# A queue of its own for gelu's derivative in a convolution and joint-network training step

## The chip, the cores and the metric

One core of a Trainium2 chip. The time is that of one execution on the device, in microseconds, host not counted. Engines: PE multiplies matrices (PEld loads its weights), DVE (VectorE) and ACT (ScalarE) work on elements, POOL (GpSimd) does so too and issues some DMAs, SP issues the others. PE writes to PSUM, which DVE and ACT empty ("evict").

## The reference

A small speech network, forward and backward. The forward part, cut to what matters:

```python
h = conv1d(x, w1, taps=3);  h = gelu(h)[:, ::2]      # T = 16000 -> 8000
f = conv1d(h, w2, taps=3);  f = gelu(f)[:, ::2]      # 8000 -> 4000
fe = f @ w_f                                         # [2, 4000, 256]
ge = g @ w_g                                         # [2, 8, 256]
j = tanh(fe[:, :, None, :] + ge[:, None, :, :])      # [2, 4000, 8, 256]
out = j @ w_o
```

`jax.vjp` then gives the gradients of all seven inputs for a given `grad_out`. Inputs and outputs are bfloat16, D = V = 256. gelu is the tanh approximation. The kernel computes it as x * sigmoid(A * (x + K x^3)) with s for the sigmoid, and its derivative as s + h * (1 - s) * (A + 3 A K x^2), where h is gelu's value.

## The kernel before, in words

**Tiling.** The 4000 time steps of the joint network are cut into chunks of 512 (`CW`), 8 per batch row, the last 416 wide, so 16 chunks in all, `n` = 0 to 15. Elements lie with the feature dimension on the 128 partitions in two halves (`KT` = 2), time along the free dimension. Because the second half of every gelu's output is thrown away, one chunk needs the first convolution at two of four input phases (`par` 0 and 1) and the second at one: three gelus a chunk, each 128 x 1024 elements.

**Order of the work.** The main loop runs over chunks. In iteration n four pairs of `u` (`up`) do the joint network of chunk n: `joint_units` gives out its work in small units. `weave` steps through these and, at a `ratio` of 0.85 units per step (0.28 in chunk 0), draws units from `fill`, a list that holds the forward half of chunk n+1 (`conv_units`, `conv2_units`, `fe_units`) and the backward half of chunk n-1 (`d1_units`, `d5_units`, `gwf_units`, `gw2_units`, `e_units`). The fill's order is: the first convolution with d1 between, d5 with gwf and gw2, then `conv2_units`, six units of e, `fe_units`, the rest of e.

**The gelu (line 196).** `gelu` returns two lists of instructions and issues none. `first` makes h: x*x, times K, (.+1)*x, the sigmoid on ACT, s*x into HT (first convolution) or FT (second). `second` makes the derivative in five DVE operations: g_sq = 3A*g_sq + A; g_x = 1 - s; g_sq *= g_x; g_sq *= h; G = g_sq + s, with G1 or G2 as the result. So g_x, g_sq and g_s live until the derivative is done. All these show as line 194 in the profile.

**The queue `later` (line 189).** The lists go into one queue, `later`, and `pump(2)`, called at each step of `weave`, issues two operations of it. For the first convolution the two `first` lists come before all ten `second` operations, with two small POOL copies of G1's border column behind (lines 259 and 263). `conv2_units` and `fe_units` begin by emptying the queue (lines 270 and 297). For chunk 0, worked in halves so that it starts sooner, the derivatives wait in a list `seconds0` and enter `later` behind the second convolution.

**Who uses the derivative.** G2 of chunk n-1 is read in iteration n by line 339 (GF), G1 by line 370 (GH). Both exist since iteration n-2. G1 and G2 have two buffers each.

**Buffers.** The pool `gel` has two of each of g_x, g_sq and g_s. `outp` has three OUT tiles of 4 KB per partition, filled by ACT (line 626) and sent by a POOL DMA (line 653) once a pair of u. `rowp` has six tiles, used by the backward transposes and, in chunk 0, by the second convolution's scratch. PSUM has seven buffers `ps` for everything but the accumulator GWO_ps.

**Other lines that matter.** 532: NGZ on DVE, out of PSUM; 524: ACT's square JSQ (two buffers), which 532 reads; 551: POOL's sum over u, ACCN and at the end NGFE; 323: DVE adds weight gradients out of PSUM (ACC); 383: copies of transposes out of PSUM (rows, JR); 313: ACT's tanh; 482: ACT's GX; 303: PE's product FE from FT.

The program is written as a stream of instructions on named tiles. The framework puts in all waits, gives out buffers, and sets the order on each engine, by the order of emission and by when it takes an instruction to be ready; engines then run in order. Only `keep_in_program_order` pins an instruction.

Of the kernel before, what the change touches and what calls it, by code (L numbers as in the profile page):

```python
# [13 lines left out]
BF16 = mybir.dt.bfloat16  # L14
FP32 = mybir.dt.float32
ALU = mybir.AluOpType
# [5 lines left out]
P = 128  # L22
KT = 2
# [4 lines left out]
CW = 512  # L28
# [3 lines left out]
def kernel(  # L32
# [22 lines left out]
    nc = tc.nc  # L55
# [7 lines left out]
    def geom(n):  # L63
        b, ci = chunks[n]
        c0 = ci * CW
        return b, ci, c0, min(CW, MQ - c0)
# [4 lines left out]
    pool = lambda name, bufs, **kw: ctx.enter_context(tc.tile_pool(name=name, bufs=bufs, **kw))  # L71
    const = pool("const", 1)
    xcp = pool("xcp", 6)
    gel = pool("gel", 2)
    htp = pool("htp", 3)
    g1p = pool("g1p", 2)
    ftp = pool("ftp", 2)
# [12 lines left out]
    jsp = pool("jsp", 2)  # L90
    ngzp = pool("ngzp", 3)
    jrp = pool("jrp", 3)
    outp = pool("outp", 3)
    tailp = pool("tailp", 1)
    PS = bass.MemoryType.PSUM
    psp = pool("psp", 7, space=PS)
# [2 lines left out]
    def ps_f32():  # L99
        return psp.tile([P, 512], FP32, name="ps", tag="ps")  # L100
# [24 lines left out]
    S = [dict() for _ in range(G)]  # L125
# [57 lines left out]
    def scratch(name, spare):  # L183
        if spare:
            return rowp.tile([P, 8, P], BF16, name="rows")[:].rearrange("p (k a) b -> p k (a b)", k=KT)
        return gel.tile([P, KT, CW], BF16, name=name)


    later = deque()

    def pump(k):
        for _ in range(k):
            if later:
                later.popleft()()  # L194

    def gelu(xb, W, h, gp, off, kts=((0, KT),), spare=False):

        sq, s = scratch("g_sq", spare), scratch("g_s", spare)
        TT, TS, STT = nc.vector.tensor_tensor, nc.vector.tensor_scalar, nc.vector.scalar_tensor_tensor
        first, second = [], []  # L200
        for (k0, k1) in kts:
            sq_, s_, x_ = sq[:, k0:k1, :W], s[:, k0:k1, :W], xb[:, k0:k1, :W]
            h_, gp_ = h[:, k0:k1, off:off + W], gp[:, k0:k1, off:off + W]
            first += [
                partial(TT, out=sq_, in0=x_, in1=x_, op=ALU.mult),
                partial(TS, out=sq_, in0=sq_, scalar1=GELU_K, scalar2=None, op0=ALU.mult),
                partial(STT, out=s_, in0=sq_, scalar=1.0, in1=x_, op0=ALU.add, op1=ALU.mult),
                partial(nc.scalar.activation, out=s_, in_=s_, func=ACT.Sigmoid, scale=GELU_A),
                partial(TT, out=h_, in0=s_, in1=x_, op=ALU.mult),
            ]  # L210
            second += [
                partial(TS, out=sq_, in0=sq_, scalar1=3.0 * GELU_A, scalar2=GELU_A, op0=ALU.mult, op1=ALU.add),
                partial(TS, out=x_, in0=s_, scalar1=-1.0, scalar2=1.0, op0=ALU.mult, op1=ALU.add),
                partial(TT, out=sq_, in0=sq_, in1=x_, op=ALU.mult),
                partial(TT, out=sq_, in0=sq_, in1=h_, op=ALU.mult),
                partial(TT, out=gp_, in0=sq_, in1=s_, op=ALU.add),
            ]
        return first, second


    HALVES = ((0, 1), (1, 2))

    seconds0 = []

    def conv_units(n):
        b, ci, c0, W = geom(n)
        seconds = []
        st = S[n]
        HT = htp.tile([P, 2, KT, CW + 2], BF16, name="HT")
        G1 = g1p.tile([P, 2, KT, CW + 2], BF16, name="G1")  # L230
        st["HT"], st["G1"] = HT, G1
        if ci == 0:
            nc.gpsimd.memset(HT[:, 1, :, 1:2], 0.0)
        else:
            nc.gpsimd.tensor_copy(out=HT[:, 1, :, 1:2], in_=S[n - 1]["HT"][:, 1, :, CW + 1:CW + 2])
        taps = {0: ((1, 0, 0), (2, 1, 0), (0, 3, -1)), 1: ((0, 1, 0), (2, 3, 0), (1, 2, 0))}
        for par in range(2):
            xb = gel.tile([P, KT, CW], BF16, name="g_x")
            for mt in range(KT):
                ps = ps_f32()  # L240
                k = 0
                for (i, c, sh) in taps[par]:
                    for kt in range(KT):
                        nc.tensor.matmul(ps[:, :W], lhsT=W1[:, i, kt, mt * P:(mt + 1) * P],  # L244
                                         rhs=st["X", c][:, kt, 16 + sh:16 + sh + W], start=(k == 0), stop=(k == 5))
                        k += 1
                nc.scalar.copy(out=xb[:, mt, :W], in_=ps[:, :W])
                yield
            first, second = gelu(xb, W, HT[:, par], G1[:, par], 2, HALVES if n == 0 else ((0, KT),))
            later.extend(first)  # L250
            seconds += second
            if n == 0:
                pump(len(first))
        if n == 0:
            seconds0.extend(seconds)
        else:
            later.extend(seconds)
        if ci > 0:
            later.append(lambda: nc.gpsimd.tensor_copy(out=G1[:, :, :, 1:2], in_=S[n - 1]["G1h"][:]))
        if ci < NCH - 1:  # L260
            st["G1h"] = halo.tile([P, 2, KT, 1], BF16, name="G1h")
            (seconds0 if n == 0 else later).append(
                lambda: nc.gpsimd.tensor_copy(out=st["G1h"][:], in_=G1[:, :, :, CW + 1:CW + 2]))

    def conv2_units(n):
        b, ci, c0, W = geom(n)
        st = S[n]
        HT = st["HT"]
        if n > 0:
            pump(len(later))  # L270
        FT = ftp.tile([P, KT, CW], BF16, name="FT")
        G2 = ftp.tile([P, KT, CW], BF16, name="G2")
        st["FT"], st["G2"] = FT, G2
        xb = scratch("g_x", n == 0)
        for mt in range(KT):
            ps = ps_f32()
            k = 0
            for (i, par, off) in ((1, 0, 2), (0, 1, 1), (2, 1, 2)):
                for kt in range(KT):
                    nc.tensor.matmul(ps[:, :W], lhsT=W2[:, i, kt, mt * P:(mt + 1) * P],  # L280
                                     rhs=HT[:, par, kt, off:off + W], start=(k == 0), stop=(k == 5))
                    k += 1
            nc.scalar.copy(out=xb[:, mt, :W], in_=ps[:, :W])  # L283
            yield
        first, second = gelu(xb, W, FT, G2, 0, HALVES if n == 0 else ((0, KT),), n == 0)
        if n == 0:
            for f in first:
                f()
            seconds0[:0] = second
            later.extend(seconds0)  # L290
        else:
            later.extend(first + second)

    def fe_units(n):
        b, ci, c0, W = geom(n)
# [386 lines left out]
    def weave(main, fill, ratio):  # L682

        due = 0.0
        for _ in main:
            pump(2)
            due += ratio
            while due >= 1.0:
                due -= 1.0
                if next(fill, StopIteration) is StopIteration:  # L690
                    due = -1e9
# [65 lines left out]
    for _ in chain(warm(16), small_units(), conv_units(0), transposed_units(), warm(4), conv2_units(0), warm(16), fe_units(0)):  # L757
        pass
# [4 lines left out]
    for n in range(G):  # L763
# [27 lines left out]
        for up in range(U // 2):  # L791
# [17 lines left out]
            if up == U // 2 - 1:  # L809
                for _ in fill:  # L810
                    pump(2)
                pump(len(later))
    n = G - 1
    gwo_rest(*prev_gwo[0], 0)
    for (o, M) in blocks(window(n)[1] - window(n)[0]):
# [2 lines left out]
        pass  # L818


    fin = gel
    for i in range(KK):
        t_ = fin.tile([P, 512], BF16, name="g_sq", tag="g_sq")
        nc.scalar.copy(out=t_[:], in_=ACC1[:, i, :])
        nc.sync.dma_start(out=out_2[i].rearrange("(dt p) n -> p dt n", p=P), in_=t_[:].rearrange("p (k n) -> p k n", k=KT))
        t_ = fin.tile([P, 512], BF16, name="g_s", tag="g_s")
        nc.vector.tensor_copy(out=t_[:], in_=ACC2[:, i, :])
        nc.sync.dma_start(out=out_3[i].rearrange("(dt p) n -> p dt n", p=P), in_=t_[:].rearrange("p (k n) -> p k n", k=KT))
    t_ = fin.tile([P, 512], BF16, name="g_x", tag="g_x")
    nc.vector.tensor_scalar(out=t_[:], in0=ACCF[:], scalar1=-1.0, scalar2=None, op0=ALU.mult)  # L830
    nc.sync.dma_start(out=out_5.rearrange("(dt p) n -> p dt n", p=P), in_=t_[:].rearrange("p (k n) -> p k n", k=KT))
    t_ = fin.tile([P, 512], BF16, name="g_x", tag="g_x")
    nc.scalar.copy(out=t_[:], in_=GWO_ps[:].rearrange("p k v -> p (k v)"))
    nc.sync.dma_start(out=out_7.rearrange("(dt p) n -> p dt n", p=P), in_=t_[:].rearrange("p (k n) -> p k n", k=KT))

# [2 lines left out]
                            in_=NGGEc[:].rearrange("p b k u c -> p (b k u) c"),  # L838
# [4 lines left out]
    for b in range(B):  # L843
# [11 lines left out]
        for dt in range(KT):  # L855
            nc.tensor.matmul(GWG_ps[:, dt * D:(dt + 1) * D], lhsT=GR8[:, b, dt * P:(dt + 1) * P],
                             rhs=ngR[:].rearrange("u kt p -> u (kt p)"),
                             start=(b == 0 and dt == 0), stop=(b == B - 1 and dt == KT - 1))
    t_ = fin.tile([P, 512], BF16, name="g_sq", tag="g_sq")
    nc.scalar.activation(out=t_[:], in_=GWG_ps[:], func=ACT.Copy, scale=-1.0)  # L860
    nc.sync.dma_start(out=out_6.rearrange("(dt p) n -> p dt n", p=P), in_=t_[:].rearrange("p (k n) -> p k n", k=KT))

# [29 lines left out]
```

## Time and profile before

| | |
|---|---|
| median of 3 runs | 883.72 us (882.99 to 883.83) |
| profiled execution | 882.75 us, of which the span is 881.0 us |
| PE, DVE, ACT, POOL busy | 833.0, 678.9, 639.0, 419.6 us |
| L194 on DVE, x*x (49 times) | 58.2 us, mean 1188 ns |
| L194 on DVE, both scalings of g_sq (98) | 67.6 us, mean 691 ns |
| L194 on DVE, 1 - s into g_x (49) | 23.2 us, mean 473 ns |
| L194 on DVE, g_sq * g_x (49) | 32.0 us, mean 653 ns |
| L194 on DVE, g_sq * HT (34) | 41.3 us, mean 1214 ns |
| L194 on DVE, sum into G (49) | 32.3 us, mean 679 ns |
| L551 on POOL, ACCN (80 + 16) and NGFE (16) | 247.6 us, mean 2.1 to 2.3 us |
| OUT's DMA (line 653), issue to landing | 3.0 / 5.5 / 10.1 us (least, median, most) |

Times are of one execution on the profiler; "busy" leaves out waiting. A row "L532 DVE ... NGZ<-JSQ,ps" is an instruction of line 532 on DVE that writes NGZ from JSQ and the PSUM tile ps, with shapes as partitions x elements. In a timeline the columns are start, duration (merged instructions from the first start to the last end), and in brackets the engine's idle time before it and whom it waited for. A regular chunk takes 52.7 us, and the chunk from 600 to 652.7 us stands for the others.

### The profile page before, as it was taken

The numbers are of one execution on the slowest core, as the hardware profiler recorded it, in microseconds if no ns is written. First come the engines' busy times: TensorE is split into PE (matmuls) and PEld (weight loads), VectorE is DVE, ScalarE is ACT, GpSimd is POOL, SyncE is SP. The second block draws the span as 40 slices with busy tenths as digits, with TensorE's granted clock in tenths as the row PEclk, the third lists the DMA queues.
The fourth block names the chain that finished last, engine by engine and source line by source line (L and its number), as shares of the span: only waits on it lengthen the run. The fifth ranks groups of instructions, "written<-read, shape, count | busy, mean of one in ns | idle before, by whom it ended". The sixth has DMA issues, their size and how long they took to land.

```text
span 881.0 us, 17824 instructions
## 1 busy us (share of the span) xinstructions
PE 833.0 (95%) x6574; PEld 600.6 (68%) x6648; DVE 678.9 (77%) x1296; ACT 639.0 (73%) x1016; POOL 419.6 (48%) x457
## 2 busy tenths in 40 slices
PE   7968999999999999998999999999999999999997
PEld 3545676767768577776756668676776757778875
DVE  5998959869596895959789596986959779596553
ACT  2767797686958769595786958768695876958534
POOL 1254544535535455553554544454554535554651
PEclk9998999999999999999999999999999999999999
DMA  9987999999999999999999999999999999997942
GB/s 207 183 182 164 191 229 233 219 210 231 239 227 229 239 179 258 196 227 214 183 197 201 250 219 224 246 230 250 198 227 225 222 237 194 229 209 175 225 136 94
DMA packets 382456, 185.67 MB, mean 211 GB/s; under 512 B 330160, under 2 KB 366280, under 8 KB 382368
## 3 DMA queue, kind: packets, MB, share of 16 engines
q1 hardware_dynamic: 362400, 114.35, 74.3%
q0 software_dynamic: 19968, 70.18, 26.9%
q8 instruction: 52, 0.85, 0.4%
q14 instruction: 36, 0.29, 0.1%
HBM read 54.43 MB, written 50.34 MB: 119 GB/s over the span
## 4 chain that ended last, share of the span: by engine, by line
PE 42%; DVE 29%; ACT 20%; issue 5%; DMA 2%; POOL 0%; ACTq 0%; POOLq 0%; DVEq 0%
DVE g_sq L194 10%; ACT JT L313 8%; PE GWO_ps L673 6%; PE ps L479 5%; PE ps L501 5%; PE ps L624 5%; DVE g_s L194 4%; PE ps L530 4%; PE ps L438 4%; PE ps L280 4%; PE pst L381 3%; DVE NGZ L532 3%; ACT GX L482 3%; DVE GH L370 3%; ACT JSQ L524 3%
## 5 line engine op out<-in xcount | busy, mean ns | idle before, releaser
L551 POOL TENSOR_TENSOR ACCN<-ACCN,NGZ 128x1024 f32<-128x1024 f32 (+1 forms) x80 | 180.3, 2254 | 174.5 <-DVE NGZ L532 173.3
L532 DVE SCALAR_TENSOR_TENSOR NGZ<-JSQ,ps 128x512 bf16<-128x512 bf16 (+1 forms) x256 | 164.2, 668 | 85.6 <-ACT GX L482 40.6
L524 ACT ACTIVATE JSQ<-JT 128x1024 bf16<-128x1024 bf16 (+1 forms) x128 | 135.3, 1059 | 76.2 <-DVE NGZ L532 76.2
L313 ACT ACTIVATE JT<-FE,GE 128x512 bf16<-128x512 f32 (+1 forms) x256 | 171.2, 738 | 0.1
L624 PE MATMUL ps<-WO,JT 128*128 128x256 bf16 x992 | 147.7, 273 | 5.7 <-DVE NGZ L532 4.9
L626 ACT CAST OUT<-ps 128x512 bf16<-128x512 f32 x248 | 143.4, 605 | 5.1 <-PE ps L624 4.7
L530 PE MATMUL ps<-GOT,WOT 128*128 128x512 bf16 (+1 forms) x472 | 134.2, 373 | 9.4 <-DVE GH L370 7.6
L673 PE MATMUL GWO_ps<-GO,JR 128*128 128x256 bf16 x992 | 139.0, 273 | 0.0
L194 ACT ACTIVATE g_s<-g_s 128x1024 bf16<-128x1024 bf16 (+2 forms) x49 | 49.3, 1005 | 98.0 <-DVE g_s L194 98.0
L624 PEld LDWEIGHTS <-JT 128*128 128x128 bf16 x992 | 94.6, 98 | 31.1 <-issue 9.5
L673 PEld LDWEIGHTS <-JR 128*128 128x128 bf16 x992 | 95.0, 98 | 23.8 <-issue 8.5
L323 DVE TENSOR_TENSOR ACC<-ACC,ps 128x512 f32<-128x512 f32 x90 | 59.2, 680 | 59.9 <-PE ps L501 55.3
L479 PE MATMUL ps<-W1T,GH 128*128 128x256 bf16 (+2 forms) x768 | 104.2, 273 | 0.4 <-ACT g_x L283 0.4
L501 PE MATMUL ps<-rows,X 128*128 128x256 bf16 (+2 forms) x768 | 92.3, 273 | 0.0
L244 PE MATMUL ps<-XC,W 128*128 128x512 bf16 (+1 forms) x370 | 88.6, 374 | 0.7 <-DMA XC<-in_x_dram 0.5
L482 ACT CAST GX<-ps 128x512 bf16<-128x512 f32 (+2 forms) x128 | 76.5, 598 | 14.1 <-PE ps L479 7.4
L479 PEld LDWEIGHTS <-GH 128*128 128x128 bf16 (+2 forms) x768 | 75.0, 99 | 15.9 <-issue 1.8
L501 PEld LDWEIGHTS <-X 128*128 128x128 bf16 (+2 forms) x768 | 74.6, 98 | 12.9 <-issue 1.3
L530 PEld LDWEIGHTS <-WOT 128*128 128x128 bf16 x512 | 49.0, 98 | 48.3 <-issue 9.5
L491 POOL DMA_DIRECT2D out_dram<-GX x64 | 35.7, 558 | 88.8 <-ACT GX L482 84.6
L653 POOL DMA_DIRECT2D out_dram<-OUT x64 | 49.4, 773 | 59.8 <-ACT OUT L626 54.7
L383 ACT COPY rows<-pst 128x1024 bf16<-128x1024 bf16 x64 | 64.2, 1013 | 10.7 <-PE pst L381 10.7
(135 smaller groups left out, 1324.0 us busy)
## 6 DMA issues: line engine op xcount, KB each, us to landing
GO<-in_grad_out_dram SPq DMA_DIRECT2D x56, 512.0 KB, 5.2
out_dram<-OUT POOLq DMA_DIRECT2D x56, 512.0 KB, 5.6
X<-in_x_dram POOLq DMA_DIRECT2D x58, 320.0 KB, 8.0
out_dram<-GX POOLq DMA_DIRECT2D x58, 256.0 KB, 3.8
JR<-JT SPq DMA_TRANSPOSE x240, 4.8
GO<-in_grad_out_dram SPq DMA_DIRECT2D x8, 384.0 KB, 4.0
out_dram<-OUT POOLq DMA_DIRECT2D x8, 384.0 KB, 4.9
GOT<-in_grad_out_dram SPq DMA_TRANSPOSE x128, 5.0
```

Source lines behind the costliest of these rows:

```text
L194: later.popleft()()
L313: nc.scalar.activation(out=JT[:, mt, :W], in_=S[n]["FE"][:, mt, :W], func=ACT.Tanh, bias=GE[:, b, mt, u:u + 1], scale=1.0)
L479: nc.tensor.matmul(ps[:Mx, cj * D:(cj + 1) * D], lhsT=GH[:, par, kt, j:j + Mx], rhs=W1T[:, i, kt, :], start=(k == 0), stop=(k == last))
L482: nc.scalar.copy(out=t[:Mx, 2 * cp:2 * cp + 2, :], in_=ps[:Mx, :])
L501: nc.tensor.matmul(ps[:, dt * D:(dt + 1) * D], lhsT=st["X5", o][:M, i + 2 * par, dt * P:(dt + 1) * P], rhs=t[:M, j + 2 * par:j + 2 * par + ...
L524: nc.scalar.activation(out=JSQ[:, :, :W], in_=JT[:, :, :W], func=ACT.Square)
L530: nc.tensor.matmul(ps[:, :W], lhsT=WOT[:, kt, mt * P:(mt + 1) * P], rhs=GOT[:, kt, :W], start=(kt == 0), stop=(kt == KT - 1))
L532: nc.vector.scalar_tensor_tensor(out=NGZ[:, mt, :W], in0=JSQ[:, mt, :W], scalar=1.0, in1=ps[:, :W], op0=ALU.subtract, op1=ALU.mult, accum_ ...
L551: nc.gpsimd.tensor_tensor(out=out, in0=in0, in1=st["NGZ", u][:, :, :W], op=ALU.add)
L624: nc.tensor.matmul(ps[:M, j * V:(j + 1) * V], lhsT=st["JT", u][:, kt, o:o + M], rhs=WO[:, kt, :], start=(kt == 0), stop=(kt == KT - 1))
L626: nc.scalar.copy(out=OUT[:M, k, :], in_=ps[:M, :])
L673: nc.tensor.matmul(GWO_ps[:, dt, :], lhsT=JR[:M, k, j, dt, :], rhs=GO[:M, k, j * V:(j + 1) * V], start=(n_gwo[0] == 0), stop=(n_gwo[0] == ...
```

## The change

The derivatives get a queue of their own, `lazy`. It is drawn from only when `later` is empty and once a second convolution has been emitted (`lazy_on`); then with one operation per step of `weave` (a step that begins with something in `later` still issues two). It is emptied at the end of each iteration, behind `later`, and switched off until the next second convolution; it is on from chunk 0's second convolution to the end of iteration 0. The second operation writes 1 - s into the result tile in place of g_x, so that g_x is free as soon as h is made. g_sq and g_s move to a pool with three buffers each; OUT loses its third. Chunk 0's first convolution takes its g_sq and g_s from `rowp`, and `seconds0` goes. At the end of the kernel the output staging tiles use the new pools.

```diff
     gel = pool("gel", 2)
+    gel3 = pool("gel3", 3)
...
-    outp = pool("outp", 3)
+    outp = pool("outp", 2)
...
-        return gel.tile([P, KT, CW], BF16, name=name)
-    later = deque()
+        return gel3.tile([P, KT, CW], BF16, name=name)
+    later, lazy = deque(), deque()
+    lazy_on = [False]
     def pump(k):
         for _ in range(k):
             if later:
                 later.popleft()()
+            elif lazy and lazy_on[0]:
+                lazy.popleft()()
...
-                partial(TS, out=x_, in0=s_, scalar1=-1.0, scalar2=1.0, op0=ALU.mult, op1=ALU.add),
-                partial(TT, out=sq_, in0=sq_, in1=x_, op=ALU.mult),
+                partial(TS, out=gp_, in0=s_, scalar1=-1.0, scalar2=1.0, op0=ALU.mult, op1=ALU.add),
+                partial(TT, out=sq_, in0=sq_, in1=gp_, op=ALU.mult),
...
-            first, second = gelu(xb, W, HT[:, par], G1[:, par], 2, HALVES if n == 0 else ((0, KT),))
+            first, second = gelu(xb, W, HT[:, par], G1[:, par], 2, HALVES if n == 0 else ((0, KT),), n == 0)
             later.extend(first)
             seconds += second
             if n == 0:
                 pump(len(first))
-        if n == 0:
-            seconds0.extend(seconds)
-        else:
-            later.extend(seconds)
+        lazy.extend(seconds)
         if ci > 0:
-            later.append(lambda: nc.gpsimd.tensor_copy(out=G1[:, :, :, 1:2], in_=S[n - 1]["G1h"][:]))
+            lazy.append(lambda: nc.gpsimd.tensor_copy(out=G1[:, :, :, 1:2], in_=S[n - 1]["G1h"][:]))
...
-            (seconds0 if n == 0 else later).append(
+            lazy.append(
...
-        xb = scratch("g_x", n == 0)
+        xb = gel.tile([P, KT, CW], BF16, name="g_x")
...
         if n == 0:
             for f in first:
                 f()
-            seconds0[:0] = second
-            later.extend(seconds0)
         else:
-            later.extend(first + second)
+            later.extend(first)
+        lazy.extend(second)
+        lazy_on[0] = True
...
-            pump(2)
+            pump(2 if later else 1)
...
-                pump(len(later))
+                pump(len(later) + len(lazy))
+                lazy_on[0] = False
```

More of the change, by code (lines that the diff above doesn't have):

```diff
@@ L221 @@
     HALVES = ((0, 1), (1, 2))
-    seconds0 = []
     def conv_units(n):
@@ L818 @@
         pass
-    fin = gel
     for i in range(KK):
-        t_ = fin.tile([P, 512], BF16, name="g_sq", tag="g_sq")
+        t_ = gel3.tile([P, 512], BF16, name="g_sq", tag="g_sq")
         nc.scalar.copy(out=t_[:], in_=ACC1[:, i, :])
         nc.sync.dma_start(out=out_2[i].rearrange("(dt p) n -> p dt n", p=P), in_=t_[:].rearrange("p (k n) -> p k n", k=KT))
-        t_ = fin.tile([P, 512], BF16, name="g_s", tag="g_s")
+        t_ = gel3.tile([P, 512], BF16, name="g_s", tag="g_s")
         nc.vector.tensor_copy(out=t_[:], in_=ACC2[:, i, :])
         nc.sync.dma_start(out=out_3[i].rearrange("(dt p) n -> p dt n", p=P), in_=t_[:].rearrange("p (k n) -> p k n", k=KT))
-    t_ = fin.tile([P, 512], BF16, name="g_x", tag="g_x")
+    t_ = gel.tile([P, 512], BF16, name="g_x", tag="g_x")
     nc.vector.tensor_scalar(out=t_[:], in0=ACCF[:], scalar1=-1.0, scalar2=None, op0=ALU.mult)
     nc.sync.dma_start(out=out_5.rearrange("(dt p) n -> p dt n", p=P), in_=t_[:].rearrange("p (k n) -> p k n", k=KT))
-    t_ = fin.tile([P, 512], BF16, name="g_x", tag="g_x")
+    t_ = gel.tile([P, 512], BF16, name="g_x", tag="g_x")
     nc.scalar.copy(out=t_[:], in_=GWO_ps[:].rearrange("p k v -> p (k v)"))
@@ L858 @@
                              start=(b == 0 and dt == 0), stop=(b == B - 1 and dt == KT - 1))
-    t_ = fin.tile([P, 512], BF16, name="g_sq", tag="g_sq")
+    t_ = gel3.tile([P, 512], BF16, name="g_sq", tag="g_sq")
     nc.scalar.activation(out=t_[:], in_=GWG_ps[:], func=ACT.Copy, scale=-1.0)
```

## The prediction

> **What bounds the kernel now.** I read the page first: engine totals, then the chain that ended last.
>
> ```profile
> span 881.0 us, 17824 instructions
> PE 833.0 (95%) x6574; PEld 600.6 (68%) x6648; DVE 678.9 (77%) x1296; ACT 639.0 (73%) x1016; POOL 419.6 (48%) x457
> PE 42%; DVE 29%; ACT 20%; issue 5%; DMA 2%; POOL 0%; ACTq 0%; POOLq 0%; DVEq 0%
> ```
>
> PE is nearly full, so a change that removes no matmul can win only PE's idle time, 881.0 - 833.0 = 48 us. DVE is second in the chain: it is where that idle time comes from. Next the table of busy time by stretch, over one regular chunk (600 to 652 us, repeated every 52.7 us), in eighths; columns are the stretch, its length, then busy time (instructions) of PE, PEld, DVE, ACT, POOL, the granted clock, the DMA share and GB/s.
>
> ```profile
> 605.60:612.20 6.60, 6.47 (x44) 4.16 (x44) 5.96 (x9) 5.99 (x11) 2.61 (x3) 1.00 1.11 271
> 612.20:618.70 6.50, 5.63 (x47) 3.49 (x46) 6.43 (x12) 2.73 (x4) 0.77 (x1) 1.00 1.09 278
> 618.70:625.30 6.60, 6.24 (x65) 5.17 (x64) 6.60 (x15) 5.47 (x8) 3.93 (x2) 1.00 1.16 142
> ...
> 638.50:645.10 6.60, 6.55 (x52) 4.95 (x52) 5.63 (x13) 6.52 (x12) 1.99 (x3) 1.00 0.95 176
> 645.10:651.70 6.60, 6.60 (x61) 5.74 (x59) 1.98 (x4) 6.60 (x12) 4.60 (x4) 1.00 1.16 305
> 651.70:658.20 6.50, 6.45 (x39) 3.73 (x39) 2.21 (x7) 6.50 (x12) 3.36 (x7) 1.00 1.17 185
> ```
>
> PE loses time in two stretches only, and there DVE is full (6.43 of 6.50, 6.60 of 6.60). Behind the second convolution DVE has 0.97 + 4.62 + 4.29 = 9.9 us free. Then PE's timeline names what it waited for:
>
> ```profile
> 617.47 0.38 PE L530 MATMUL ps<-GOT,WOT 128*128 128x512 bf16 x1 [0.65 <-DVE GH L370]
> 618.07 1.03 PE L367 MATMUL ps<-GF,W2T 128*128 128x512 bf16 x4 [0.22 <-DVE rows L383]
> 619.29 0.60 PE L624 MATMUL ps<-WO,JT 128*128 128x256 bf16 x4 [0.19 <-DVE NGZ L532]
> ...
> 621.10 0.49 PE L381 MATMUL pst<-ident,HT 128*128 128x128 bf16 x6 [0.16 <-DVE GH L370]
> ```
>
> Each is a PSUM bank, or a tile, that DVE hands on late. A matmul is drawn some 0.16 us longer than its share (128x256 takes 0.27 us, the next starts 0.11 us later), so a gap is longer than its bracket by that. Start to start I get 0.81 + 0.38 + 0.36 + 0.18 + 0.32 = **2.05 us a chunk** between 616.6 and 621.1. Last, what DVE does meanwhile that nobody there needs (line 194 is a helper's, which is the gelu):
>
> ```profile
> 611.06 0.42 DVE L194 TENSOR_SCALAR g_sq<-g_sq 128x1024 bf16<-128x1024 bf16 x1
> ...
> 612.39 0.43 DVE L194 TENSOR_SCALAR g_x<-g_s 128x1024 bf16<-128x1024 bf16 x1
> 612.86 0.69 DVE L194 TENSOR_TENSOR g_sq<-g_sq,g_x 128x1024 bf16<-128x1024 bf16 x1
> ...
> 619.76 0.69 DVE L194 TENSOR_TENSOR g_sq<-g_sq,HT 128x1024 bf16<-128x1024 bf16 x1
> ...
> 621.57 1.16 DVE L194 TENSOR_SCALAR g_sq<-g_sq 128x1024 bf16<-128x1024 bf16 x1
> 622.65 0.41 DVE L194 TENSOR_SCALAR g_x<-g_s 128x1024 bf16<-128x1024 bf16 x1
> ```
>
> These are derivatives (`second`) of the first convolution's gelus. Their results G1 are used a whole chunk later.
>
> **Part 1: the derivative moves behind the second convolution.** DVE runs in order. Ahead of the last GH (624.19) it now runs, by distance of starts, 0.34 + 0.46 + 0.60 + 0.61 + 1.08 + 0.33 + 0.60 (the product at 623.59) = 4.0 us of derivative. The order on the engine is not the order of emission (the row at 611.06 runs ahead of the gelu's own last step), so a later emission alone proves little. A buffer does: after the change operations 2 to 5 write G1, which has two buffers, and the one they take is read by those same GHs until 624. So 0.46 + 0.60 + 0.61 + 0.33 + 0.60 = 2.6 us must leave; the two first operations (0.34, 1.08) may stay. GH at 616.73 then comes 0.46 + 0.60 = 1.06 us earlier, as does the rows copy behind it: the gaps of 0.81 and 0.38 go. NGZ behind them comes 1.06 earlier, but PE comes 1.19 earlier: of 0.36 some 0.3 stays. The last two gaps (0.18, 0.32) are behind the 0.61 that also leaves: I count 0.2 of their 0.50 as kept. Won: 2.05 - 0.5 = 1.55; for an order in which the two early operations do harm I take off 0.2: **1.35 us a chunk**. There are 14 chunks with both a forward and a backward half: 14 x 1.35 = **19 us**. Bounds: 14 x 2.05 = 29 us if every gap goes; below nothing if the work hurts where it lands.
>
> **Where it lands.** Ten operations, 2 x (2 x 0.43 + 3 x 0.68) = 5.8 us, go to the 9.9 us that DVE has free behind the second convolution: counted at nothing. The cover is that free time. Queued behind them on DVE are NGZ (line 532), ACC (line 323) and their PSUM banks; without the cover PE waits for those, and ACT's next square (line 524) for JSQ's buffer.
>
> An uncertain part is POOL. The row at 624.79, a product of 0.68 us, took 2.02 while POOL's ACCN addition ran (623.81 to 626.26). Over the whole trace 62 derivative or gelu operations were held like that, 79.8 us in all, 1.29 each, against 112 additions. Emitted singly, more of them meet an addition: at most 50 more, 50 x 1.29 / 16 = 4.0 us a chunk. 5.8 + 4.0 = 9.8 still fits in 9.9, barely; at the least nothing is added. I take it as hidden.
>
> The Trainium skill speaks against the change here (SBUF — State Buffer, section "Who interferes with whom"): a VectorE instruction with two SBUF inputs and a GpSimd one that reads SBUF exclude each other for the whole instruction, and the loser fully blocks. The trace bears that out for the 2.02 us row, but not always: the two-input step that makes g_s, 1.21 us, was held in none of 49 cases, since it starts on the heels of another. By the rule alone every addition holds one operation, the 4.0 us above; by the trace, four of seven in the chunk shown.
>
> The second operation now writes 1-s into G1 instead of g_x, a row the trace lacks: between 0.43 (to g_x) and 0.68 (a product into G1), so 0 to 0.5 us a chunk; I take 0.43, the same kind of operation; it lies in the same free time.
>
> **Part 2: the queue's pace, and POOL.** Five gelu steps no longer have ten derivative steps in the same queue; `first` keeps two per joint unit. The two halo copies of G1 (0.33 and 0.21 us) move with it in POOL's queue and wait there for DVE; behind them stand ACCN and output DMAs. NGFE ends at 596.5 and is first used at 605.1: 8.6 us cover, so nothing; without it, line 337 starts late. SP's queue is passed by nothing.
>
> **Part 3: buffers.** A third pair g_sq/g_s (4 KB) is paid for with OUT's third buffer (4 KB). OUT's DMA leaves at 602.89 and lands after 5.5 us (at most 10.1); with two buffers the first ACT write that needs it is at 620.90, 18 us later: nothing. Were that gone, ACT would wait in line 626. The first chunk's scratch comes from `rows`, six buffers for six tiles, idle until 87 us: nothing.
>
> **Part 4: chunk 0.** From 40 to 75 us DVE is never idle, and PE waits for it:
>
> ```profile
> 60.00:75.00 15.00, 9.58 (x66) 6.78 (x66) 14.86 (x25) 7.16 (x12) 8.81 (x6) 0.77 0.58 146
> 69.46 1.01 PE L303 MATMUL ps<-FT,WF 128*128 128x512 bf16 x2 [5.37 <-DVE FT L194]
> ```
>
> The wait of 5.37 also costs clock (granted 0.77 in that stretch; half from 66.5 to 73.3, about 1.9 us of matmuls). Chunk 1's first-convolution derivative (starts 51.97 to 57.80, 4.9 us) goes behind FT; of chunk 0's own (6 halves x 1.42 = 8.5 us, now done by 33 to 37) part goes into the crowded stretch instead. Best: 10 us of idle between 40 and 75 plus 1.9 = 12; worst: -3, the part of the 8.5 that finds no gap. Nearer to the lower end, as DVE stays full: **3 us**.
>
> **Sum.** 882.75 (profiled execution: span 881.0 and 1.75 around it) - 19 - 3 = 860.8. The runs' median, 883.72, is 1.0 above that execution: **862 us**.
>
> **Rivals.**
>
> *The wait moves into ACT's busy stretch, and the kernel is slower.* From 639 to 610 ACT is full (6.52 of 6.60, 6.60 of 6.60) with tanh, squares and evictions in one order. If derivative operations held by POOL stand ahead of NGZ, ACT's square waits for JSQ (two buffers; that wait is already 76.2 us in the kernel), and evictions behind it are late. Two additions lie there (644.43, 647.09) and one at the next chunk's start: 3 x 1.29 = 3.9 us late, less some 1.5 that seven PSUM banks absorb = 2.4 a chunk against 1.35 won: 14 x 1.05 = 15 slower, 883.7 + 15 - 3 = 895. It decides from 22 / 14 = 1.6 us a chunk on. For it: ACT is full there. Against: DVE's own idle gaps in that stretch are 3.07 and 3.77 us long, ready for low-priority work.
>
> *The derivative stays in the first half.* If the order on DVE barely changes, nothing is won: 881 to 885. Against: G1's buffer, above.
>
> *Only part of PE's wait goes,* because another DVE operation is late next: half of 1.35, no gain in chunk 0: 883.7 - 9 = 874. For it: DVE still has gelus, GH, rows and NGZ there.
>
> **How the numbers follow.** The forecast (850 to 868): 0.52. A partial gain (868 to 882): 0.16. The derivative staying: 0.07. Slower: 0.25, half of it above 891. A measurement of this kernel tells about 0.2% (1.8 us) from no change. Faster 0.68, same 0.07, slower 0.25. The likeliest case's own range is 850 to 868; for 8 in 10, the low end is every gap and half of chunk 0's best, 883.7 - 29 - 7 = 847, the high end reaches into the slower rival: 893.
>
> **What would show it.** Right: PE's idle time between GH and the transposes under 0.7 us a chunk, chunks about 51.3 us apart, L194 rows between 640 and 658 us of such a chunk. Chunk 0: PE's wait before line 303 under 3 us. Wrong: waits of PE for ACT's GX, OUT or g_x, ACT's square waiting longer than 76 us, or a chunk pitch of 52.7 with gaps behind the second convolution.

## The result and the profile after

The changed kernel takes **868.29 us** (median of 4 runs, 867.94 to 868.67) beside 883.36 us (4 runs of the kernel before): ratio 0.9832 with a 95% interval of 0.9814 to 0.985, 15.1 us less. The profiled execution took 868.67 us, 14.1 less than that of the kernel before. Now and then an execution of any of these kernels is over 1.5% longer at a lower granted clock; medians here are over all executions, the ratios leave those out, so the two can differ a little. The page of the changed kernel, its span, engine totals and chain:

```profile
span 866.8 us, 17881 instructions
PE 832.0 (96%) x6648; PEld 598.9 (69%) x6648; DVE 668.5 (77%) x1296; ACT 639.3 (74%) x1016; POOL 413.4 (48%) x457
PE 44%; DVE 25%; ACT 22%; DMA 4%; issue 4%; POOL 0%; ACTq 0%; POOLq 0%; DVEq 0%
```

PE does the same work (6648 matmuls). By the pages its idle time fell from 48.0 to 34.8 us, but the page of before holds only 6574 of the matmuls, so the 48.0 is too high: the profile of e3 (below, the kernel before with two OUT tiles) holds them all and shows 884.3 - 841.5 = 42.8 us. DVE's share of the chain fell from 29 to 25%. Next the table by stretch of the changed kernel for the same chunk, which now starts some 11.7 us earlier (columns as before: stretch, length, PE, PEld, DVE, ACT, POOL, clock, DMA share, GB/s):

```profile
593.90:600.50 6.60, 6.43 (x44) 4.08 (x43) 5.52 (x9) 6.33 (x11) 3.08 (x4) 1.00 1.09 388
600.50:607.00 6.50, 6.13 (x51) 3.75 (x49) 6.47 (x12) 3.06 (x5) 0.82 (x1) 1.00 1.04 286
607.00:613.60 6.60, 6.55 (x73) 5.76 (x71) 6.60 (x13) 6.32 (x9) 6.18 (x6) 1.00 1.29 158
613.60:620.20 6.60, 6.60 (x47) 4.03 (x45) 6.60 (x14) 0.70 (x2) 1.44 (x4) 1.00 1.08 205
...
633.40:640.00 6.60, 6.60 (x63) 5.91 (x62) 1.34 (x4) 6.60 (x12) 4.36 (x5) 1.00 1.48 264
```

The two stretches in which PE lost time now give it 6.13 of 6.50 and 6.55 of 6.60 (5.63 and 6.24 before; one matmul of 0.22 us is missing from the 5.63, see below). DVE is as full there as it was: the work on it was put in another order, not taken away. PE's timeline of the changed kernel (start, duration, in brackets the idle time and its releaser) shows what is left, and the wait in chunk 0:

```profile
64.93 0.59 PE L302 MATMUL ps<-FT,WF 128*128 128x512 bf16 x2 [2.78 <-DVE FT L196]
...
599.60 0.38 PE L366 MATMUL ps<-GF,W2T 128*128 128x512 bf16 x1 [0.17 <-DVE GF L338]
...
605.07 0.60 PE L529 MATMUL ps<-GOT,WOT 128*128 128x512 bf16 x2
606.03 1.03 PE L366 MATMUL ps<-GF,W2T 128*128 128x512 bf16 x4 [0.37 <-DVE rows L382]
```

The wait of L529 for GH (0.65 before) is gone; the one for the rows copy is now the longest, 0.53 us start to start; the one for GF is 0.33. Two short ones follow, 0.22 between products of L437 and 0.11 ahead of L302. And the DVE timeline of the same chunk (merged rows run from the first start to the last end):

```profile
595.74 1.50 DVE L196 TENSOR_TENSOR g_sq<-g_x 128x1024 bf16<-128x1024 bf16 x1 [0.82 <-ACT g_x L249]
...
599.47 0.42 DVE L198 TENSOR_SCALAR g_sq<-g_sq 128x1024 bf16<-128x1024 bf16 x1
...
604.08 0.68 DVE L369 TENSOR_TENSOR GH<-ps,G 128x512 bf16<-128x512 f32 x1
604.69 0.69 DVE L196 TENSOR_TENSOR HT<-g_s,g_x 128x1024 bf16<-128x1024 bf16 x1
605.29 0.68 DVE L382 COPY rows<-pst 128x1024 bf16<-128x1024 bf16 x1
...
608.92 0.69 DVE L369 TENSOR_TENSOR GH<-ps,G 128x512 bf16<-128x512 f32 x1
609.52 0.42 DVE L198 TENSOR_SCALAR g_sq<-g_sq 128x1024 bf16<-128x1024 bf16 x1
609.86 2.69 DVE L198 TENSOR_SCALAR G<-g_s 128x1024 bf16<-128x1024 bf16 x2
612.46 1.28 DVE L198 TENSOR_TENSOR g_sq<-g_sq,G 128x1024 bf16<-128x1024 bf16 x2
613.67 1.28 DVE L198 TENSOR_TENSOR g_sq<-g_sq,HT 128x1024 bf16<-128x1024 bf16 x2
614.87 0.68 DVE L322 TENSOR_TENSOR ACCF<-ACCF,ps 128x512 f32<-128x512 f32 x1
615.47 1.28 DVE L198 TENSOR_TENSOR G<-g_sq,g_s 128x1024 bf16<-128x1024 bf16 x2
...
621.90 0.69 DVE L196 TENSOR_TENSOR g_sq<-g_x 128x1024 bf16<-128x1024 bf16 x1 [0.32 <-ACT g_x L282]
```

Line 198 is now the derivative, line 196 the gelu itself. Nine of the ten derivative operations run in one clump directly behind the last GH (608.92); one scaling, at 599.47, stays in front. They are not spread at one per joint unit, and they don't wait for the second convolution's gelu, which starts at 621.90. The operations that write G stand right behind the last reader of the old G1.

**Where the 14.2 us of span came from.** The first d1 product of chunk 0 (from NGFE) starts at 76.28 in place of 79.12: 2.84 us. The other 11.3 came later, chunk by chunk: a regular chunk takes 51.75 in place of 52.68 us, 0.93 less.

**A correction to the gaps.** The profile of before lacks 74 of 6648 matmuls, 40 of them of line 530 (472 of 512); those of e9 to e12 lack the same 74, all the others none. The gap of 0.38 us behind GH that the prediction counted is one of the places where a record is missing: its row there (617.47) shows one matmul, the row of after at 605.07 shows two. A matmul of 512 columns is 0.217 us, so the real gap was 0.165; e3's profile, which lacks none, shows 0.164 there. With that, the PE gaps of a regular chunk (over 0.04 us, start to start) add up for each kernel, and their differences agree with those of the pitch (start of one chunk to the next) within 0.02 us:

| kernel | GF | GH | rows | NGZ, pst | behind | sum | pitch |
|---|---|---|---|---|---|---|---|
| before | 0.24 | 0.81 | 0.165 | 0.355 + 0.176 + 0.325 | 0.07 | 2.14 | 52.68 |
| after | 0.33 | 0 | 0.53 | 0 | 0.22 + 0.11 | 1.19 | 51.75 |
| e1, 1 - s into G alone | 0.35 | 0 | 0.53 | 0 | 0.22 + 0.05 + 0.53 + 0.24 | 1.92 | 52.47 |
| e3, before, two OUT tiles | 0.24 | 0.82 | 0.165 | 0.355 + 0.175 + 0.33 | 0.07 | 2.15 | 52.69 |
| e2, queue alone | 0.23 | 0.81 | 0.17 | 0.355 + 0.175 | 0.32 | 2.06 | 52.61 |
| e5, queue drawn at once | 0.34 | 0 | 0.53 | 0 | 0.22 + 0.05 + 0.53 + 0.23 | 1.90 | 52.44 |
| e4, rows copies on ACT | 0.23 | 0 | 0 | 0 | 0.10 + 0.69 | 1.02 | 51.58 |
| e8, second rows copy on ACT | 0.23 | 0 | 0.10 | 0 | 0.43 | 0.77 | 51.32 |
| e10, before, no additions | 0 | 0.35 | 0.165 | 0.355 + 0.175 + 0.325 | 0 | 1.37 | 51.92 |
| e7, after, no additions | 0.06 | 0 | 0 | 0 | 0.22 | 0.28 | 50.84 |
| e12, before, half additions | 0.05 | 0.81 | 0.165 | 0.355 + 0.175 + 0.96 | 0.30 | 2.82 | 53.37 |
| e11, after, half additions | 0.06 | 0 | 0.53 | 0 | 0.22 | 0.81 | 51.36 |

In e10, e11 and e12 the same record is missing; the 0.38 us seen in e10 and e12 and the 0.75 us in e11 are put down without it.

### The profile page after: what moved, and what is told of

Same layout as the page of the kernel before. It is cut to its first block, busy times and chain, and to the rows that moved or that the text cites. A ratio compares the mean times of both kernels' runs of the same rounds, so it can differ in the third digit from the quotient of the medians.

```text
span 866.8 us, 17881 instructions
## 1 busy us (share of the span) xinstructions
PE 832.0 (96%) x6648; PEld 598.9 (69%) x6648; DVE 668.5 (77%) x1296; ACT 639.3 (74%) x1016; POOL 413.4 (48%) x457
## 4 chain that ended last, share of the span: by engine, by line
PE 44%; DVE 25%; ACT 22%; DMA 4%; issue 4%; POOL 0%; ACTq 0%; POOLq 0%; DVEq 0%
ACT JT L312 7%; PE ps L529 6%; DVE g_sq L196 6%; PE GWO_ps L672 5%; DVE NGZ L531 5%; PE ps L478 5%; PE ps L500 5%; ACT JSQ L523 5%; PE ps L623 4%; PE ps L279 4%; PE pst L380 4%; DVE g_s L196 4%; PE ps L437 4%; PE ps L366 3%; ACT rows L382 3%
## 5 line engine op out<-in xcount | busy, mean ns | idle before, releaser
L550 POOL TENSOR_TENSOR ACCN<-ACCN,NGZ 128x1024 f32<-128x1024 f32 (+1 forms) x80 | 174.3, 2178 | 146.0 <-DVE NGZ L531 143.5
L312 ACT ACTIVATE JT<-FE,GE 128x512 bf16<-128x512 f32 (+1 forms) x256 | 173.2, 755 | 0.1
L529 PE MATMUL ps<-GOT,WOT 128*128 128x512 bf16 (+1 forms) x512 | 138.4, 374 | 0.0
L196 ACT ACTIVATE g_s<-g_s 128x1024 bf16<-128x1024 bf16 (+1 forms) x45 | 46.6, 1035 | 67.8 <-DVE g_s L196 67.8
L246 PE MATMUL ps<-XC,W 128*128 128x512 bf16 (+1 forms) x384 | 91.2, 375 | 2.1 <-DVE JR L382 1.2
L529 PEld LDWEIGHTS <-WOT 128*128 128x128 bf16 x512 | 48.5, 98 | 39.1 <-issue 0.6
```

The lines of the kernel that those rows point to most:

```text
L312: nc.scalar.activation(out=JT[:, mt, :W], in_=S[n]["FE"][:, mt, :W], func=ACT.Tanh, bias=GE[:, b, mt, u:u + 1], scale=1.0)
L529: nc.tensor.matmul(ps[:, :W], lhsT=WOT[:, kt, mt * P:(mt + 1) * P], rhs=GOT[:, kt, :W], start=(kt == 0), stop=(kt == KT - 1))
L550: nc.gpsimd.tensor_tensor(out=out, in0=in0, in1=st["NGZ", u][:, :, :W], op=ALU.add)
```

## The experiments

Ratios compare with runs of the kernel before on the same chip, with 95% intervals.

### Which part of the change does it: e1 and e2

e1 is the kernel before with only the target of 1 - s changed:

```diff
-                partial(TS, out=x_, in0=s_, ...
-                partial(TT, out=sq_, in0=sq_, in1=x_, op=ALU.mult),
+                partial(TS, out=gp_, in0=s_, ...
+                partial(TT, out=sq_, in0=sq_, in1=gp_, op=ALU.mult),
```

e2 is the changed kernel with these two lines the other way round, so that the queue, the pace and the buffers remain.

> The kernel before, with one edit: the derivative's second operation writes 1 - s into G1 or G2 instead of g_x. No second queue, no new buffers. Theory A (G1's buffer, not the queue, holds the derivative back until the last GH has read the old G1): regular chunks as after the whole change, 51.75 us apart instead of 52.66, chunk 0 as before (line 337 of the first backward half at about 79 us), so 883.4 - 11 = 872 us. Theory B (the late place in the queue does it): 883 us, chunks 52.66 us apart.

> The changed kernel, but 1 - s goes into g_x as before; the second queue, its place and its pace stay. Theory A: chunk 0 keeps its gain of about 2.8 us and regular chunks are as before the change (52.66 us apart), so 883.4 - 3 = 880 us. Theory B: as the changed kernel, 868 us. Between (each alone moves most of the same operations): 870 to 875 us.

**Measured:** e1 880.44 us, 0.9961 (0.9944 to 0.9977); e2 879.02 us, 0.9941 (0.9921 to 0.9962). Neither is the change: the parts win some 3 and 5 us, both together 15. e2 is where its theory A had it (880), e1 between its two theories (872 and 883). Ahead of the last GH of a chunk the kernel before runs seven derivative operations. In the trace of e1 five of them leave, as G1's buffer forces them to, but one of the two that stay, the scaling of phase 1, stands ahead of the last GH and meets a POOL addition there. The timeline of e1, on DVE, ACT and PE, and ACT's same square in the changed kernel (last row):

```profile
617.74 1.44 DVE L194 TENSOR_SCALAR g_sq<-g_sq 128x1024 bf16<-128x1024 bf16 x1
...
619.71 0.68 DVE L370 TENSOR_TENSOR GH<-ps,G 128x512 bf16<-128x512 f32 x1
620.42 2.26 DVE L194 TENSOR_SCALAR G<-g_s 128x1024 bf16<-128x1024 bf16 x2
...
629.20 0.68 DVE L532 SCALAR_TENSOR_TENSOR NGZ<-JSQ,ps 128x512 bf16<-128x512 bf16 x1
...
629.98 1.06 ACT L524 ACTIVATE JSQ<-JT 128x1024 bf16<-128x1024 bf16 x1 [6.59 <-DVE NGZ L532]
...
631.56 0.82 PE L479 MATMUL ps<-W1T,GH 128*128 128x256 bf16 x6 [0.37 <-ACT g_x L283]
...
619.85 1.06 ACT L523 ACTIVATE JSQ<-JT 128x1024 bf16<-128x1024 bf16 x1 [5.89 <-DVE NGZ L531]
```

A 0.42 us scaling takes 1.44, what follows it on DVE is late (counted from the chunk's second GF, the NGZ at 629.20 comes 0.70 us later than in the changed kernel), ACT's square waits 6.59 us for that NGZ in place of 5.89, and the eviction behind the square (g_x) keeps a PSUM bank from PE. That is a gap of 0.53 the kernel before doesn't have, with 0.24 at L303 behind it. In e2 it is the other way round. Of the seven, the later emission moves four, but the first three (scaling, 1 - s and their product, 1.4 us) stay ahead of the first two GH, and PE's waits (total, times, longest; the last row) are as before there:

```profile
610.90 0.43 DVE L198 TENSOR_SCALAR g_x<-g_s 128x1024 bf16<-128x1024 bf16 x1
611.37 0.69 DVE L198 TENSOR_TENSOR g_sq<-g_sq,g_x 128x1024 bf16<-128x1024 bf16 x1
...
612.58 0.69 DVE L369 TENSOR_TENSOR GH<-ps,G 128x512 bf16<-128x512 f32 x1
...
PE ps L529 <- DVE GH L369: 7.5, 12, 0.9
```

A later emission did not by itself make those three run later. With 1 - s in G1 two of them have to: 1 - s can't be written before the last GH has read the old G1, and in e1 both 1 - s start right behind that GH (619.71, 620.42). The scaling, which doesn't touch G1, stays. Why e2 keeps just these three early was not tried; they are also the ones up to the last read of g_x, a tile that the second convolution needs. e2 keeps the gain in chunk 0 (first d1 at 76.20), which e1 lacks (79.63).

### Is it the place of the emission: e5

The changed kernel, with its queue drawn as soon as `later` is empty, and two operations per step:

```diff
-            elif lazy and lazy_on[0]:
+            elif lazy:
...
-            pump(2 if later else 1)
+            pump(2)
```

> The changed kernel, but the second queue is drawn from as soon as `later` is empty, from the first convolution on, two operations a step: neither the place behind the second convolution nor the pace of one is left. Theory C (what the place in the queue wins in a regular chunk is that the first derivative operation of phase 1, the scaling of g_sq, no longer runs ahead of the last GH, where a POOL addition holds it): that operation comes back in front, chunks as in the run with the target alone (about 52.4 us apart), 868.3 + 14 x 0.6 = 877 us. Rival (the pace and place do nothing, the pair of g_sq/g_s buffers or the fresh scratch did the rest): 868 us.

**Measured:** 879.05 us, 0.9937 (0.9915 to 0.9959), near theory C's 877 and far from the rival's 868. The gaps of a regular chunk are e1's to 0.02 us, and the scaling is again ahead of the last GH, held by POOL (1.44 us at 618.88). So, with the buffer given, the place and the pace move one operation that counts in a regular chunk, the first scaling of phase 1, and that is worth 52.44 - 51.75 = 0.69 us a chunk. In chunk 0 the place counts too: the first d1 product starts at 78.45, so 2.17 of the 2.84 us are gone.

### The covers taken as free: e3 and e6

e3 is the kernel before with two OUT tiles; e6 is the changed kernel without the third g_sq and g_s:

```diff
-    outp = pool("outp", 3)
+    outp = pool("outp", 2)
...
-    gel3 = pool("gel3", 3)
+    gel3 = pool("gel3", 2)
```

> The kernel before with two OUT buffers in place of three, nothing else. By the prediction's part 3 the buffer is needed 18 us after its transfer starts: 883.4 us, within 1 us. If two buffers do cost something, ACT's line 626 shows a wait for the transfer of OUT, and the time is over 885 us; the change would then have won more without it.

> The changed kernel with two buffers of g_sq and g_s in place of three. If the derivative is done before the second convolution's gelu begins, as the trace of the changed kernel has it (617 and 622 us), the third buffer is worth nothing: 868 us, chunks 51.75 us apart. If the derivative really waits behind the second convolution, the gelu there stands behind it: over 872 us.

**Measured:** e3 883.66 us, 0.9995 (0.9977 to 1.0014); e6 866.75 us, 0.9793 (0.9767 to 0.9819), with the changed kernel's gaps and pitch. Its profiled execution took 878.51 us and had waits for DMAs in some chunks (last section). Both third buffers are worth nothing that can be measured; two scratch tiles do for the new queue.

### What POOL's additions cost: e7 and e10

Six of the seven additions of NGZ per chunk are left out (NGFE is the sum of the last two NGZ), in the changed kernel (e7) and in the kernel before (e10):

```diff
-        if u == 0:
+        if u < U - 1:
             return
...
+        in0 = st["NGZ", u - 1][:, :, :W]
```

> The changed kernel without six of seven additions of a chunk on POOL: NGFE is NGZ of the last two u alone, so the gradients behind it lack the others; all else stays. If DVE operations held by POOL's additions make up what is left of PE's wait, that wait falls from 1.2 to under 0.6 us a chunk and DVE's held time from 72 to about 10 us: 868.3 - 14 x 0.6 = 860 us or less. If not, 866 to 868 us.

> The kernel before without six of seven additions of a chunk on POOL (as in the run of the changed kernel without them; NGFE is NGZ of the last two u alone). Theory D (PE's wait before the change is the derivative's own time plus what POOL holds it; the change takes away the one and not the other): PE still waits for GH, 0.8 to 1.2 us a chunk instead of 2.1, about 883.5 - 14 x 1.1 = 868 us, slower than the changed kernel without additions (853 to 862). Rival (POOL's holds are all of it, and the derivative's place would not matter without them): 853 to 862 us, as that one.

**Measured:** e7 859.46 us, 0.9749 (0.97 to 0.9797), its profiled execution 853.43; e10 860.40 us, 0.9728 (0.9699 to 0.9757). DVE's held time falls to 1.6 and 1.8 us: the additions are what holds DVE. PE's waits of e10:

```profile
PE ps L530 <- DVE GH L370: 3.9, 11, 1.0
PE ps L303 <- DVE FT L194: 2.4, 1, 2.4
PE ps L367 <- DVE rows L383: 2.0, 9, 0.3
PE ps L620 <- DVE NGZ L532: 2.0, 9, 0.5
```

and of e7:

```profile
PE GWO_ps L668 <- DMA JR<-JT: 6.5, 6, 2.2
...
PE ps L302 <- DVE FT L196: 0.8, 1, 0.8
```

Without the holds the derivative still delays GH, the rows and NGZ in the kernel before, 1.37 us a regular chunk, and nothing of that is left in a regular chunk of the changed one. So the waits are as theory D said, but e10's time is not: 860.40 us lies in the rival's 853 to 862, not at D's 868, and the medians and ratios of e7 and e10 do not tell the two apart. By the pitch the change wins 51.92 - 50.84 = 1.08 us a chunk there, against 0.93 with the additions. Over 14 chunks that would be 15 us, but the spans are only 7.4 apart (859.1 and 851.7): e7 has a new wait of 6.5 us, in which PE stands before GWO until a transposing DMA of JT (JR) has landed. So what the change is worth without additions is shown by the regular chunk alone. Leaving out the additions saves the kernel before more (23 us of its median) than the change does.

### The wait that is longest now: e4 and e8

The copies of transposes that feed the weight gradient of w_f move from DVE to ACT, both of them (e4), or the second alone (e8):

```diff
-            transposes(srcs, dsts)
+            transposes(srcs, dsts, nc.scalar.copy)
```

and

```diff
-            transposes(srcs, dsts)
+            transposes(srcs, dsts, nc.scalar.copy if k else None)
```

> The changed kernel, with the copies of the transposed FT and NGFE (rows, in gwf_units) out of PSUM done by ACT instead of DVE: two copies a chunk, 0.68 us each on DVE. If DVE's lateness is what is left of PE's wait (0.53 us a chunk before line 366 falls to it), chunks come 51.2 to 51.4 us apart: 868.3 - 14 x 0.45 = 862 us. If ACT is as late there (its sigmoids wait for DVE in the same stretch), 868 us or slower.

> The changed kernel, with only the second of the two rows copies of FT and NGFE on ACT. With both on ACT PE no longer waited 0.53 us for DVE's copy but 0.69 us for ACT's later copies before line 437. If one copy fits into ACT's idle time and the other does not, both waits shrink: PE idle under 0.8 us a chunk, 868.3 - 14 x 0.4 = 863 us. If ACT's lateness behind line 437 comes from the second copy, as with both: 866 us.

**Measured:** e4 866.51 us, 0.9801 (0.9769 to 0.9833), not told apart from the change itself. PE's longest wait of e4:

```profile
PE ps L437 <- ACT rows L382: 6.5, 11, 1.0
```

The gap of 0.53 is gone, and one of 0.69 behind ACT has come: 0.17 us a chunk is won. e8 is inconclusive: 875.63 us, 0.9832 (0.9774 to 0.9889), with runs of 862.95 and 864.68 and others of 875.58 to 881.29. In its profiled execution of 875.67 PE waits 10.4 us for JR's DMA (transposes of JT that GWO needs), as here in PE's timeline:

```profile
554.68 0.28 PE L672 MATMUL GWO_ps<-GO,JR 128*128 128x256 bf16 x1 [2.52 <-DMA JR<-JT]
556.28 0.28 PE L672 MATMUL GWO_ps<-GO,JR 128*128 128x256 bf16 x1 [1.32 <-DMA JR<-JT]
```

What the copy on ACT is worth in all cannot be read from such times. A regular chunk without such a wait can be read: its gaps are down to 0.77 us and its pitch to 51.32, 0.43 less than the changed kernel, as the expectation's "under 0.8" and 0.4 had it.

### Shorter holds: e9, e11 and e12

Each POOL addition is cut into two of half the size, in the changed kernel (e11) and in the kernel before (e12); e9 is the changed kernel again, on the same chip:

```diff
-        nc.gpsimd.tensor_tensor(out=out, in0=in0, in1=st["NGZ", u][:, :, :W], op=ALU.add)
+        for kt in range(KT):
+            nc.gpsimd.tensor_tensor(out=out[:, kt], in0=in0[:, kt], in1=st["NGZ", u][:, kt, :W], op=ALU.add)
```

> The changed kernel once more, unaltered, to stand beside the other three on the same chip: 868 us, 0.983 of the kernel before.

> The changed kernel with every addition on POOL cut into two of half the size, the same sums. A held DVE operation then waits for at most one half (1.07 us) before its turn. If the length of one addition sets the price: held time of DVE from 72 to some 40 us, PE's wait in a regular chunk from 1.2 to 0.7, 868.3 - 14 x 0.5 = 861 us. If POOL's second half gets in again before DVE, or halves cost POOL more than they save: 868 us or more.

> The kernel before with the same cut of POOL's additions, nothing of the change: held time of DVE from 80 to some 45 us, 35 / 16 = 2.2 us a chunk that DVE has more while it is full, of which PE gets about half of its 2.1 us back: 883.5 - 14 x 0.9 = 871 us. If the derivative's own time is what PE waits for: 880 us or more.

**Measured:** e9 869.86 us, 0.9834 (0.9798 to 0.9871); e11 865.41 us, **0.9756** (0.9718 to 0.9793); e12 887.12 us, 1.0045 (1.0016 to 1.0073). e11 is the fastest version that computes everything, though its interval only just clears that of e9 and overlaps those of e4 and e6. It lies between its two expectations (861 and 868). The GF gap falls from 0.33 to 0.06, the pitch to 51.36. e12 is a miss: DVE's held time fell from 79.8 to 54.9 us, and the kernel is slower by 0.45%. Its DVE timeline, and then its POOL's and PE's, tell why:

```profile
621.37 1.32 DVE L194 TENSOR_TENSOR g_sq<-g_sq,HT 128x1024 bf16<-128x1024 bf16 x1
622.62 0.68 DVE L370 TENSOR_TENSOR GH<-ps,G 128x512 bf16<-128x512 f32 x1
...
621.00 2.71 POOL L552 TENSOR_TENSOR ACCN<-ACCN,NGZ 128x512 f32<-128x512 f32 x2 [5.24 <-DVE NGZ L532]
...
623.35 0.49 PE L381 MATMUL pst<-ident,HT 128*128 128x128 bf16 x6 [0.80 <-DVE GH L370]
```

In the kernel before this product started at 619.76, 0.24 us ahead of the addition (620.00), and took 0.69. Half an addition can start on half an NGZ (in e12 at 621.00, before the second half of NGZ is done), so it is 0.37 us ahead of the product, which takes 1.32. GH behind it is 0.64 late, and PE's gap there grows from 0.325 to 0.96. This agrees with the Trainium skill (SBUF — State Buffer, section "Who interferes with whom"), by which the order of issue decides which of the two is blocked. Total held time says little, then: 0.64 us a chunk in front of GH cost more than 25 us less held time in all gave back.

## Why the prediction was right, and where it was off

**Direction and mechanism: right.** 868.3 us lies in the range of 847 to 893 and 6 above the forecast of 862; it is 0.3 above the upper end of the likeliest case's own range, so by the number alone it falls just inside the rival "only part of PE's wait goes", and that rival's reason is part of the truth: the rows copy is late next. Of the signs named, the gap between GH and the transposes is 0.53 (under 0.7), the pitch of 51.75 lies between the 51.3 for right and the 52.7 for wrong. What the change does in front of GH is what Part 1 said: G1's buffer, not the later emission, takes the derivative from in front of the GH that PE waits for (it is gone in e1, with the buffer alone, and stays in e2, with the queue alone). From the last GF ahead of it to the second GH it is 604.08 - 598.87 = 5.21 us, before 616.73 - 610.46 = 6.27: the 1.06 us of the prediction.

**The term that was mis-sized is the 1.35 us a chunk;** it measured 0.93. By its own parts: of the 2.05 us of gaps, 0.217 was a missing record (the row with "x1" could have told it); the upper bound of 48 us for PE's idle time was too high for the same reason. Kept were 0.53 where 0.50 was said, but all of it in one place, before the rows: HT went in front of the second rows copy, which came 6.87 - 6.42 = 0.45 us earlier (from GF, as above) and not 1.06. And the harm outside that stretch was 0.09 + 0.15 + 0.11 = 0.35, not 0.2. So 2.05 - 0.22 - 0.53 - 0.35 = 0.95. POOL's holds account for some of it: without them a regular chunk wins 1.08. Over the 14 chunks 11.3 us came in place of 19, less than 14 x 0.93 = 13, since not every chunk is regular: between starts of FE the gain runs from -0.6 to 1.9 us.

**"The two first operations may stay", with 0.2 for the harm: half wrong.** That of phase 0 stays and harms nothing that shows. That of phase 1 had to go: where it stays (e1, e5) it costs 0.69 to 0.72 us a chunk, by a chain the prediction knew only as a rival, NGZ late, ACT's square, the eviction behind it.

**Where it lands: the place was wrong, the price right.** The clump lies from 609.52 to 616.7, ahead of ACC and the second convolution's gelu (with one ACCF addition in it), not behind that convolution, where the prediction looked for it (640 to 658 us of the old chunk). PE is busy 6.55 and 6.60 of 6.60 us while it runs, and its one gap there, 0.22, is put down to ACT's rows copy: nothing that PE needs in those 7 us is seen to wait behind the clump on DVE.

**POOL's holds: right that they would not decide, wrong that they might rise.** Held operations fell from 62 to 48 and held time from 79.8 to 72.2 us, against the same 112 additions. In a clump, additions meet a run of operations of which they hold few: two additions, from 607.34 to 611.92, held one of the two 1 - s operations, which take 0.42 each and here 2.69 us together. The prediction took the Trainium skill's rule to mean that every addition holds one operation. The page (same section as above) says that whichever issues first blocks the other, so an addition can be the one that waits; here 48 operations were held against 112 additions.

**Buffers, POOL's queue, 1 - s into G1: right.** e3 and e6 show the buffers; no engine waits for a halo copy in the profile; the operation writing G1 takes 0.415 us where it isn't held. ACT's wait for NGZ rose to 79.0 us; the bound of 76 us named for a failure was the value before, too close to mean anything.

**Chunk 0: right,** 2.84 us for 3, and PE's wait 2.78 us for "under 3". That it came so close is partly luck: the 3 was picked between -3 and 12, and it is the rest of two larger terms. Chunk 1's product FE starts 4.53 us earlier (64.93 in place of 69.46), and 1.7 of that is lost again before the first d1 product. The table by stretch of the changed kernel:

```profile
60.00:75.00 15.00, 9.88 (x72) 6.20 (x71) 15.00 (x29) 10.42 (x17) 8.30 (x10) 1.00 1.12 201
```

The granted clock is 1.00 (0.77 before): an idle time of 2.78 us does not cost clock here, one of 5.37 did. The Trainium skill (TensorE: Matmul & The Clock Gate, Part 1) puts the line at a window of about 3.4 us, which fits both.

**The slower rival** (ACT late, 895) had the right chain and the wrong place: it happens at the last GH in e1 and e5, and takes away most of the gain of a regular chunk there, but not more than it.

## What to carry to other kernels

Where a framework orders the work, ask which buffer an operation must wait for before asking where it is emitted: of seven operations that stood in the way the buffer alone moved five (e1), the later emission alone four (e2), and both together six; each alone left something behind that cost most of what the rest had won. Try the parts of a change together as well as alone, since waits in series hide each other: here the parts gave 0.4 and 0.6%, both 1.7%. Price a held operation by what stands behind it on its engine, not by the sum of held time; and check that each gap in a timeline is a wait and not a record that is missing, by the count of instructions in the same row of another kernel.

## What the runs showed of the hardware

**Late transposing DMAs.** In some profiles PE waits for JR, the transposing DMA from SBUF to SBUF: 6.5 us in all in e7, 10.4 in e8, 5.6 in e11 and 5.1 in e6. There is none of it in the others, e10 among them, which is as fast as e7. Each version has one profile, so whether the wait goes with the version or with the execution is not known. The median time from issue to landing is 5.4 us in the changed kernel, 5.3, 5.1, 5.3 and 5.1 in e7, e8, e11 and e6. The longest ones don't tell the profiles apart either: 17.2 us in e8, but 17.3 in e3, which has no such wait. In e8 the clock fell behind the wait. Its table by stretch

```profile
553.00:556.60 3.60, 0.56 (x2) 0.19 (x2) 3.60 (x4) 2.50 (x4) 2.64 (x3) 1.00 1.44 134
556.60:560.00 3.40, 3.24 (x20) 2.56 (x21) 1.99 (x4) 1.10 (x2) 0.38 (x2) 0.50 1.23 236
```

shows PE nearly idle around the two waits above, and half the clock granted in the 3.4 us that follow. Times of one kernel can differ by 8 us: 866.03 to 873.91 in e9 (867.94 to 868.67 in the first four executions of the same kernel). Its profile, of the 873.91, shows another late DMA, one that sends out GX: ACT waits 4.65 us for it and PE then 2.68 us for ACT, at 181 us. Why those transfers are late was not tried and stays open.

**Cutting an instruction in two can cost.** Half-size additions on POOL left DVE less held time (54.9 in place of 79.8 us in e12), and with them the changed kernel is faster (0.9756 beside 0.9834) and the kernel before slower (1.0045).
